# One PSUM pool of eight banks, five sets of seven products in each later group, and a tabled order, in a fused attention and gated FFN kernel

## The chip, the cores and the metric

The kernel runs on one core of a Trainium2 chip. The metric is device time in microseconds for one execution. The kernel before takes 313.35 us, the median of three runs from 313.17 to 313.43.

The engines are named as in the profile: PE is TensorE (PEld are its weight loads), DVE is VectorE, ACT is ScalarE, POOL is GpSimd, SP is the engine that issues most DMAs.

## The reference

Four batches, eight heads, 768 tokens, head size 64. Each query and key is assigned to the nearest of 16 centroids of its head; a query attends only to keys of its own cluster. The heads' outputs, side by side, are the 3072 x 512 input of an FFN with a sigmoid gate and 1536 hidden columns.

```python
q_assign = np.argmax(np.einsum('bhsd,hcd->bhsc', q_n, c_n), axis=-1)
k_assign = np.argmax(np.einsum('bhsd,hcd->bhsc', k_n, c_n), axis=-1)
mask = q_assign[:, :, :, None] == k_assign[:, :, None, :]
scores = np.where(mask, scale * np.matmul(q, k.transpose(0, 1, 3, 2)), -1000000000.0)
attn = np.exp(scores - np.max(scores, axis=-1, keepdims=True))
attn = attn / (np.sum(attn, axis=-1, keepdims=True) + 1e-09)
x = np.matmul(attn, v)          # then (b, s, h*d)
out = (1 / (1 + np.exp(-(x @ w_gate))) * (x @ w_val)) @ w_out
```

## The kernel before

**Attention.** Heads go in pairs. A pair's queries and keys are transposed (on PE at first, L617, L795, L903, later on DVE, L595), cast to 16 bits on POOL, and given 16 more rows that hold the one-hot cluster; a score matmul over 80 rows (L1008) thus adds the mask. The cluster scores come from L687, L835 and L948. An exponential on ACT (L1032) takes two score products of 384 columns at once out of two banks and writes them to one of four `es` tiles; there are 189 exponentials. The value products (L1059) take `es` as stationary operand against 65 columns of v and a column of ones, so that the sum comes with them. DVE divides (L1084, L1089), and a DMA, or PE in some blocks (L1097), transposes the result into `x`.

**FFN.** Tokens are worked in eight groups (b, gr), two of each batch, of 384 tokens (of 256 and 512 in the first batch). For each of 12 chunks of 128 hidden columns there are four matmuls with the gate weights and four with the value weights over all tokens of the group (`proj`, L1389, L1396); ACT takes tanh out of the gate's bank (L1561), DVE multiplies into `hT` (L1572). The output projection (`project`, L1186, matmuls at L1271) does two blocks of 128 tokens at a time with seven half-size products in place of eight. The sigmoid is had from tanh of half the argument.

**Seven products.** `seven_products` (L1445) does two neighbouring chunks of gate and value at once: a 2 x 2 block product with seven block products in place of eight. The blocks are halves of the input rows (`d`) and halves of the tokens (192). It needs sums of the weights, made once on DVE (`sum_up_weights`, L1366, four for each pair of chunks, in `wss`), and four differences of `x` for each group (`t_tasks`, L1436). A set is seven products of four matmuls of 192 columns (L1474), three copies out of PSUM on ACT (L1493), three additions on DVE (L1505), two tanh on ACT (L1512) and two gates on DVE (L1520). A pair of chunks done in the plain way is 16 matmuls of 384 columns, two tanh and two gates. Three banks X, Y, Z are held in a set, and X for nearly all of it: m1, copy, m6, copy, m7, addition, m4, gate. The pairs start at chunks `WP = (2, 4, 8)`; by group the kernel does 0, 0, 2, 2, 2, 3, 3, 2 sets, 14 in all. In the last group X and Y are the two banks of one score buffer.

**What sets the order.** Every piece of work is a task with an engine, an estimated duration, tasks it depends on, tile buffers (`Buf`) that it acquires or uses, and a due time. `Order.schedule` (L129) plans all tasks in a list schedule: on each engine, of those that can start within 0.02 us of the earliest, the one that is due first. The plan only fixes the order in which instructions stand on each engine, and which buffer each takes; engines then run their instructions in that order and wait on semaphores. `run` (L119) plans nine times, with DMA landing times from `transfers` (L94) between. Due times come from formulas (L319, L322).

**PSUM.** The eight banks are divided: `sc` is two buffers of two banks for scores, `av` one bank for value products, `ring` three banks for all else (L246). Buffers of `sc` and `av` are taken in turn, of `ring` the one that is free first (L70).

**DMA queues.** SP issues the loads of k, q and v (L334), the copies of half the rows to the other tile (`odd<-even`, L654), the cluster rows (`oht`), the transposes of x (L1117) and the stores; POOL issues the weights, v of later batches and some k and q.

Of the kernel before, what the change touches and what calls it, by code (L numbers as in the profile page):

```python
# [9 lines left out]
FP = mybir.dt.float32  # L10
# [3 lines left out]
AX = mybir.AxisListType  # L14

# [23 lines left out]
class Order:  # L39
# [30 lines left out]
    def free_slots(self, tag, count):  # L70

        held, got = self.held[tag], self.taken[tag]
        ends = []
# [10 lines left out]
        if tag in self.ANY:  # L84
            ends = sorted(x for x in ends if x[0] is not None)
        else:
            n = len(got) % len(held)
            ends = (ends + ends)[n : n + count]
# [5 lines left out]
    def transfers(self):  # L94


        begin = self.DMA_START
        todo = sorted((t for t in self.tasks if t.dma), key=lambda t: t.start + begin[t.eng])
        queues, left, now, n = {}, {}, 0.0, 0
        while n < len(todo) or any(queues.values()):  # L100
            heads = [ts[0] for ts in queues.values() if ts]
            come = todo[n].start + begin[todo[n].eng] if n < len(todo) else float("inf")
            if heads:
                total = sum(t.pkt for t in heads)
                step = min(min(left[t] * total / t.pkt for t in heads), max(0.0, come - now))
                for t in heads:
                    left[t] -= step * t.pkt / total
                    if left[t] < 1e-6:
                        t.landing = now + step + self.DMA_LAND - t.start
                        queues[t.eng].remove(t)  # L110
                now += step
            else:
                now = max(now, come)
            while n < len(todo) and todo[n].start + begin[todo[n].eng] <= now + 1e-9:
                queues.setdefault(todo[n].eng, []).append(todo[n])
                left[todo[n]] = todo[n].dma
                n += 1

    def run(self):  # L119

        for _ in range(8):
            order = self.schedule()
            self.transfers()
        order = self.schedule()
        for t in order:
            t.emit()
        return order

    def schedule(self):  # L129
# [10 lines left out]
        while any(wait.values()):  # L140
            best = None
            for e, ts in wait.items():
                cand = []
                for t in ts:
                    r = t.ready
                    for tag in {b.tag for b in t.acq}:
                        f = self.free_slots(tag, sum(b.tag == tag for b in t.acq))[0]
# [18 lines left out]
            wait[t.eng].remove(t)  # L166
            free[t.eng] = start + t.dur
# [21 lines left out]
            for tag in dict.fromkeys(b.tag for b in t.acq):  # L189
                mine = [b for b in t.acq if b.tag == tag]  # L190
                for b, slot in zip(mine, self.free_slots(tag, len(mine))[1]):
# [18 lines left out]
def kernel(  # L210
# [45 lines left out]
        "xn": ([128, QCH, 128], HP), "x": ([128, NDC, 512], HP), "hT": ([128, NFC, 512], HP),  # L256
        "gt": ([128, 512], FP), "p5": ([128, 384], FP), "out2": ([128, 2, DM], FP),
        "sc": ([128, 2, 512], FP), "av": ([128, 512], FP), "ring": ([128, 512], FP),
    }
    PSUM = bass.MemoryType.PSUM  # L260
    SPACES = {"sc": PSUM, "av": PSUM, "ring": PSUM}
# [4 lines left out]
            (banks if tag in SPACES else const).tile(*SHAPES[tag], name=f"{tag}{i}")  # L266
            for i in range(n)
        ]
        for tag, n in BUFS.items()
    }  # L270
    for tag, (of, which) in HEIRS.items():
# [5 lines left out]
    def take(buf):  # L277
        buf.tile = kept[buf.tag][buf.slot]
        return buf.tile

# [12 lines left out]
    WP = (2, 4, 8)  # L293
    wss = const.tile([128, len(WP), 4, 2, 2, 128], HP, name="wss")
# [56 lines left out]
    w_ring = Buf("av")  # L351
# [66 lines left out]
    c_ring = Buf("av")  # L418
# [160 lines left out]
    def prepare(b, grp, due, step, act=(), queues=("SP",), split=False):  # L579
# [101 lines left out]
        rg = Buf("sc")  # L681

        def scored():
            ps = take(rg)
# [9 lines left out]
            due, lat=0.3, acq=[rg], uses=[t32[x] for x in sides],  # L694
        )
        for half in range(2):
# [10 lines left out]
            def back(cols=cols, oh=oh, half=half):  # L707
# [5 lines left out]
                lambda t1=t1, half=half: turn_scores(take(t1)[:n], rg.tile[:n, half, :QB]),  # L713
                [cl], due, lat=0.11, acq=[t1], uses=[rg],
# [268 lines left out]
    def attend(block, at, slot):  # L983
# [11 lines left out]
        sc, es = Buf("sc"), Buf("es")  # L995
# [714 lines left out]
```

## Time and profile before

| | us |
|---|---|
| median of three runs | 313.35 |
| the profiled execution | 313.22 |
| its span, first to last instruction | 311.4 |
| busy PE, ACT, DVE, POOL in the span | 303.7, 238.2, 217.8, 77.0 |
| DMA, mean rate over the span | 111 GB/s |

The view by stretches gives for each window of the span how long each engine was busy, then the granted clock (1.00 is full), the share of the DMA engines and GB/s. The groups give, behind line, engine and operation, output and inputs with their shapes, count, then busy time and mean duration of one in ns, and the idle time before. Recorded durations of one engine overlap, so what an instruction takes from its engine is read from start to start in the timeline (start, duration), or from the chain, where each piece stands with the time it adds. Weight loads run beside matmuls.

### The profile page before, as it was taken

To read this page: it belongs to the slowest core of one execution; us is meant where nothing else is said; L and a number is where in the kernel's file an instruction comes from. 1 tells how busy PE (TensorE), PEld (TensorE's weight loads), DVE (VectorE), ACT (ScalarE), POOL (GpSimd) and SP (SyncE) were. 2 spreads that over 40 slices of the span, in tenths; PEclk is the share of its full clock that TensorE was granted. 3 is DMA by queue.
4 is the path that set the end of the run, shared out by engine and by line. 5 is a ranking of instruction groups with operands and counts; after the bars stand their busy time and mean duration, and the time that the engine had idled before them with its cause. 6 is when DMAs were issued, how large, how long until landed. Compare 5 with 4: busy or idle time off the path is not lost.

```text
span 311.4 us, 8300 instructions
## 1 busy us (share of the span) xinstructions
PE 303.7 (98%) x3251; PEld 222.8 (72%) x3251; DVE 217.8 (70%) x532; ACT 238.2 (76%) x389; POOL 77.0 (25%) x110
## 2 busy tenths in 40 slices
PE   8998999999999999999999999999999999999995
PEld 3676888544687867757776877757777888778784
DVE  4999945899865739885376938977375824685862
ACT  4799999334999989868997777959899778945531
POOL 4997756751012302440002200570000000000000
PEclk9999999999999999999999999999999999999999
DMA  6999999993356966891465673978300121001003
GB/s 217 359 272 212 214 175 129 163 154 72 69 99 142 114 100 204 106 114 45 107 105 84 101 182 99 103 101 73 96 4 14 48 83 46 15 2 67 2 1 135
DMA packets 97286, 34.49 MB, mean 111 GB/s; under 512 B 83120, under 2 KB 93024, under 8 KB 97248
## 3 DMA queue, kind: packets, MB, share of 16 engines
q1 hardware_dynamic: 72192, 24.57, 34.6%
q0 software_dynamic: 24336, 8.65, 26.4%
q10 hardware_dynamic: 720, 0.75, 0.7%
q8 instruction: 25, 0.41, 0.6%
q14 instruction: 13, 0.11, 0.2%
HBM read 28.34 MB, written 6.29 MB: 111 GB/s over the span
## 4 chain that ended last, share of the span: by engine, by line
PE 92%; ACT 4%; DVE 1%; DMA 1%; issue 0%; SPq 0%; ACTq 0%
PE ring L1396 29%; PE sc L1008 19%; PE ring L1271 16%; PE av L1059 11%; PE ring L1474 9%; ACT es L1032 3%; PE sc L687 3%; PE sc L1271 1%; PE sc L1474 1%; DMA nat<-in_k_dram 1%; PE ring L795 1%; PE ring L617 1%; PE ring L835 1%; PE ring L903 0%; PE ring L948 0%
## 5 line engine op out<-in xcount | busy, mean ns | idle before, releaser
L1032 ACT ACTIVATE es<-sc,nbias 128x768 f16<-128x768 f32 (+1 forms) x189 | 167.8, 925 | 21.2 <-PE sc L1008 20.4
L1059 PEld LDWEIGHTS <-es 128*128 128x128 f16 x1152 | 53.6, 97 | 13.6
L1059 PE MATMUL av<-vp,es 128*128 128x65 f16 x1152 | 58.6, 193 | 0.0
L1396 PE MATMUL ring<-x,wv 128*128 128x384 f16 (+2 forms) x272 | 55.4, 326 | 0.1
L1396 PE MATMUL ring<-x,wg 128*128 128x384 f16 (+2 forms) x272 | 55.3, 326 | 0.0
L1561 ACT ACTIVATE gt<-ring 128x384 f32<-128x384 f32 (+2 forms) x68 | 33.9, 499 | 28.0 <-PE ring L1396 24.8
L1572 DVE SCALAR_TENSOR_TENSOR hT<-gt,ring 128x384 f16<-128x384 f32 (+2 forms) x68 | 37.2, 548 | 24.3 <-PE ring L1396 20.7
L650 POOL CAST even<-t 128x768 f16<-128x768 f32 x24 | 20.6, 875 | 119.9 <-DVE t L595 47.1
L1396 PEld LDWEIGHTS <-wv 128*128 128x128 f16 x272 | 24.7, 97 | 16.5 <-issue 2.1
L1396 PEld LDWEIGHTS <-wg 128*128 128x128 f16 x272 | 24.4, 97 | 14.6 <-issue 0.8
L1271 PEld LDWEIGHTS <-hT 128*128 128x128 f16 x294 | 27.3, 97 | 5.0
L1008 PE MATMUL sc<-even 80*128 80x384 f16 (+2 forms) x120 | 26.1, 293 | 1.6 <-ACT es L1032 0.9
L1008 PE MATMUL sc<-odd 80*128 80x384 f16 x96 | 26.6, 325 | 0.1
L1271 PE MATMUL ring<-wo,hT 128*128 128x256 f16 x198 | 26.4, 272 | 0.0
L1008 PE MATMUL sc<-even,odd 80*128 80x384 f16 (+2 forms) x120 | 26.1, 293 | 0.0
L1008 PE MATMUL sc<-odd,even 80*128 80x384 f16 x96 | 25.8, 326 | 0.0
L1008 PEld LDWEIGHTS <-even 80*128 80x128 f16 x216 | 19.7, 98 | 8.2 <-issue 3.1
L1008 PEld LDWEIGHTS <-odd 80*128 80x128 f16 x216 | 19.7, 98 | 7.3 <-issue 2.1
L595 DVE STREAM_TRANSPOSE t<-nat 128x384 f32<-128x384 f32 x40 | 21.1, 553 | 1.2 <-DMA nat<-in_q_dram 0.9
L1505 DVE TENSOR_TENSOR nat<-ring,nat 128x384 f32<-128x384 f32 x26 | 13.9, 548 | 10.8 <-ACT nat L1493 9.2
L1296 DVE SCALAR_TENSOR_TENSOR out<-ring,diff 128x256 f32<-128x256 f32 x22 | 9.3, 422 | 17.0 <-PE ring L1271 16.8
L1271 PEld LDWEIGHTS <-s 128*128 128x128 f16 x198 | 18.7, 97 | 3.4
(133 smaller groups left out, 444.8 us busy)
## 6 DMA issues: line engine op xcount, KB each, us to landing
out_dram<-out SPq DMA_DIRECT2D x22, 256.0 KB, 2.2
nat<-in_k_dram SPq DMA_DIRECT2D x32, 96.0 KB, 3.0
nat<-in_q_dram SPq DMA_DIRECT2D x32, 96.0 KB, 3.0
odd<-even SPq DMA_DIRECT2D x12, 192.0 KB, 2.9
vp<-in_v_dram POOLq DMA_DIRECT2D x24, 96.0 KB, 4.6
nat<-in_k_dram SPq DMA_DIRECT2D x5, 384.0 KB, 7.7
nat<-in_q_dram SPq DMA_DIRECT2D x5, 384.0 KB, 6.2
nat<-in_v_dram SPq DMA_DIRECT2D x4, 384.0 KB, 7.9
```

Source lines behind the costliest of these rows:

```text
L595: nc.vector.transpose(t[:, half * QB : (half + 1) * QB].rearrange("p (c x) -> p c x", x=128), blocks_[:, half],)
L650: nc.gpsimd.tensor_copy(t[:, NM[nm], cols], t32[p, nm].tile[:, cols])
L687: nc.tensor.matmul(out=ps[32 * g : 32 * g + 32, half, :QB], lhsT=cblk[:, 2 * p + half, :], rhs=t32[p, nm].tile[:, half * QB : (half + 1) * ...
L1008: nc.tensor.matmul(out=to, lhsT=kb.tile[0:80, 0, e * QB + j // 2 * 128 : e * QB + (j // 2 + 1) * 128], rhs=qb_.tile[0:80, 1, e * QB + c0 * ...
L1032: i = nc.scalar.activation(to, of, AF.Exp, bias=nbias, scale=D ** -0.5 if quarters(b, p) else scale,).ins
L1059: nc.tensor.matmul(out=av.tile[:, g : g + D + 1], lhsT=es.tile[:, i * N + c * 128 : i * N + (c + 1) * 128], rhs=vp[:, e, j, :], start=firs ...
L1271: nc.tensor.matmul(out=ps[:, lo:hi], lhsT=left_()[:, i], rhs=right(i)[:, lo:hi], start=new and i == 0, stop=i == NFC // 2 - 1, skip_group_ ...
L1396: nc.tensor.matmul(out=ps[:, :N], lhsT=ws[fc // FPG][:, dcc, fc % FPG, :], rhs=xb.tile[:, dcc, :N], start=(dcc == 0), stop=(dcc == NDC - 1),)
L1474: nc.tensor.matmul(out=ps[:, f], lhsT=w_[:, d, f], rhs=x_()[:, d], start=new and not (f or d), stop=d == 1, skip_group_check=True,)
L1505: lambda: nc.vector.tensor_tensor(held(i), bank(r_, y), held(i), ALU.add), deps,
L1561: lambda rg=rg, gt=gt: nc.scalar.activation(take(gt)[:, :N], rg.tile[:, :N], AF.Tanh, scale=0.5),
L1572: nc.vector.scalar_tensor_tensor(t[:, fc, :N], gt.tile[:, :N], 1.0, rv.tile[:, :N], ALU.add, ALU.mult)
```

## The change

Three things change together.

1. **PSUM.** All eight banks form `ring`. A single bank is the free one whose neighbours are least useful as a pair; scores, and the cluster scores of L687, take any two neighbouring banks. `sc` (2) and `av` (1) stay as turns without memory: still at most two score pairs and one value bank are under way. The last group's sets and projections use single banks as well.
2. **Five sets** for each group of the batches 1 to 3 (`WP = (2, 4, 6, 8, 10)`), none in batch 0: 30 sets. To make room for the sums of five pairs, one of the four sums of each (g1 - v1) is written over the value weights v1 themselves, after the last plain product that reads them (`raw_users`), and the first `hT` tile is cut from 512 to 384 columns.
3. **The order.** The due times are no longer formulas: `PLACES` gives every task a rank, and `LANDINGS` every DMA a planned time; `transfers` goes. `schedule` keeps its rules, so buffers and dependencies work as before.

The numbers of instructions that differ, in the built programs: matmuls of L1396 with 384 columns 352 to 96, matmuls of L1474 392 to 840 (weight loads alike), copies of L1493 42 to 90, L1512 28 to 60, L1561 with 384 columns 44 to 12, additions of L1505 42 to 90, gates of L1520 28 to 60, L1572 with 384 columns 44 to 12, weight sums 12 to 20. Nothing else differs in number; the DMAs of SP, ACT and POOL are the same ones in another order.

```diff
...
+            till = [float("inf") if e is None else e for e, _ in ends]
+            if count == 2:
+                pairs = [(max(pair), i) for i, pair in enumerate(zip(till, till[1:]))]
+                end, i = min(pairs)
+                return (None, None) if end == float("inf") else (end, [i, i + 1])
+            soon = max(min(till), now)
+            beside = [min(till[max(i - 1, 0) : i] + till[i + 1 : i + 2]) for i in range(len(till))]
+            i = max((i for i, e in enumerate(till) if e <= soon), key=lambda i: (beside[i], -i))
+            return (None, None) if till[i] == float("inf") else (till[i], [i])
...
-        for _ in range(8):
-            order = self.schedule()
-            self.transfers()
+        places, landings = ([float(x) for x in text.split()] for text in (PLACES, LANDINGS))
+        moved = [t for t in self.tasks if t.dma]
+        assert len(places) == len(self.tasks) and len(landings) == len(moved)
+        for t, at in zip(self.tasks, places):
+            t.due = at
+        for t, landing in zip(moved, landings):
+            t.landing = landing
         order = self.schedule()
...
-        "sc": 2, "av": 1, "ring": 3, "p5": 2,
+        "ring": 8, "p5": 2, "sc": 2, "av": 1,
...
-    WP = (2, 4, 8)
-    wss = const.tile([128, len(WP), 4, 2, 2, 128], HP, name="wss")
+    WP = (2, 4, 6, 8, 10)
+    wss = const.tile([128, len(WP), 3, 2, 2, 128], HP, name="wss")
...
-        sc, es = Buf("sc"), Buf("es")
+        turn_, sc, es = Buf("sc"), [Buf("ring") for _ in range(2)], Buf("es")
...
-            avb[block] = Buf("av")
-        av = avb[block]
+            avb[block] = Buf("ring"), Buf("av")
+        av, in_av = avb[block]
...
-            r1, r2 = Buf("sc"), Buf("sc")
-            X, Y, Z = (lambda: r1.tile[:, 0, :HM]), (lambda: r2.tile[:, 0, :HM]), (lambda: r1.tile[:, 1, :HM])
...
+        r1, r2 = Buf("ring"), Buf("ring")
+        X, Y, Z = (lambda: r1.tile[:, :HM]), (lambda: r2.tile[:, :HM]), (lambda: r1.tile[:, HM:])
...
-        for to, x, y, op in (
-            (s1, v1, v2, ALU.add), (s3, g1, v1, ALU.subtract), (s2, s1, g1, ALU.subtract), (s4, g2, s2, ALU.subtract),
+        for to, x, y, op, raw in (
+            (s1, v1, v2, ALU.add, []), (s2, s1, g1, ALU.subtract, []), (s4, g2, s2, ALU.subtract, []),
+            (v1, g1, v1, ALU.subtract, raw_users[fa] + raw_users[fa + 1]),
         ):
...
-        seven = WP[: {(0, 0): 0, (0, 1): 0, (1, 0): 2, (1, 1): 2, (2, 0): 2, (2, 1): 3, (3, 0): 3, (3, 1): 2}[b, gr]]
-        if (b, gr) == (B - 1, 1):
-            seven = (2, 4)
-        if not wsums_of:
+        seven = WP if b else ()
+        if seven and not wsums_of:
...
-            if (b, gr) == (B - 1, 1):
-                X = Y = Buf("sc")
-            else:
-                X, Y = Buf("ring"), Buf("ring")
-            Z = Buf("ring")
+            X, Y, Z = Buf("ring"), Buf("ring"), Buf("ring")
...
             rv, v1 = proj("v", fc, due, [g1])
+            raw_users[fc].append(v1)
...
```

More of the change, by code (lines that the diff above doesn't have):

```diff
@@ L68, in behind, with free_slots @@
             t.left += 1
[L70 removed]
+    def free_slots(self, tag, count, now=0.0):
         held, got = self.held[tag], self.taken[tag]
@@ L166, in schedule @@
             wait[t.eng].remove(t)
+            now = max(t.ready, free[t.eng])
             free[t.eng] = start + t.dur
```

126 lines of the change are left out of this document (54 added, 72 removed), and 104 rows, old and new, of tables (LANDINGS, PLACES).

## The prediction

> **What bounds the kernel now.** I read the page's busy line first, then its clock row, then the chain that ended last.
>
> ```profile
> span 311.4 us, 8300 instructions
> PE 303.7 (98%) x3251; PEld 222.8 (72%) x3251; DVE 217.8 (70%) x532; ACT 238.2 (76%) x389; POOL 77.0 (25%) x110
> PEclk9999999999999999999999999999999999999999
> PE 92%; ACT 4%; DVE 1%; DMA 1%; issue 0%; SPq 0%; ACTq 0%
> ```
>
> TensorE (PE) carries 92% of the chain at full clock. The view by stretches tells where this holds and who else is near; behind the stretch and its length stand the busy times of PE, weight loads, DVE, ACT and POOL.
>
> ```profile
> 20.00:50.00 30.00, 28.92 (x400) 23.92 (x399) 23.38 (x67) 29.68 (x42) 20.48 (x28) 1.00 1.38 187
> 60.00:80.00 20.00, 20.00 (x111) 9.02 (x110) 19.37 (x44) 8.38 (x14) 7.56 (x10) 1.00 0.92 129
> 110.00:300.00 190.00, 189.19 (x2030) 141.88 (x2029) 130.63 (x300) 149.55 (x255) 21.56 (x26) 1.00 0.44 77
> ```
>
> From 20 to 50 us ScalarE (ACT) is full (29.68 of 30): there the exponentials set the time, PE waits a little. From 110 to 300, where every group with seven-product sets is worked, PE is full and ACT and VectorE (DVE) have 40 and 59 us to spare. A busy PE is not PE at peak, so I looked in the chain for what a group of matmuls really takes, and in the waits for what stops PE:
>
> ```profile
> 119.18 0.65 PE ring L1396 x4
> 120.16 0.66 PE ring L1474 x8
> 124.01 0.37 PE av L1059 x12
> ```
>
> ```profile
> 75.20 0.86 PE ring L1396 x4
> 132.00 1.43 PE sc L687 x16
> 302.37 1.31 PE ring L1271 x12
> ```
>
> ```profile
> PE sc L1008 <- ACT es L1032: 0.9, 2, 0.5
> PE sc L1474 <- DVE nat L1505: 0.5, 1, 0.5
> ```
>
> Four matmuls of 384 columns take 0.65 us (0.1625 each), eight of 192 take 0.66 (0.0825 each): time goes by columns. The three rows of the second fence are used below: four matmuls of 512 columns, 16 of the cluster scores (L687), twelve of 256 columns (0.109 each). PE waited for an exponential for 0.9 us in all. So a column less on PE is time less, unless the work added on ACT and DVE makes PE wait.
>
> **The change, part by part.** I counted the instructions of the changed kernel, form by form, against those of before. Only this differs in number; all else is the same work in another order.
>
> PE: 256 matmuls of 384 columns go (352 become 96, L1396), 448 of 192 columns come (392 become 840, L1474). That is 14 sets of seven products before and 30 after; a set is 28 small matmuls for 16 large ones. Sum: 256 x 0.1625 = 41.6 us away, 448 x 0.0825 = 37.0 us more: **-4.6 us**. Nothing covers PE here, so all of it counts.
>
> A small matmul brings a weight load of its own, 192 more in number (448 for 256).
>
> ```profile
> L1474 PEld LDWEIGHTS <-wss 128*128 128x128 f16 x224 | 19.1, 97 | 2.8 <-issue 0.6
> ```
>
> A load is recorded with 97 ns, longer than the 82.5 of its matmul. If loads bound, the 448 would cost 448 x 0.097 = 43.5, and the part would be +1.9 us. But eight pairs already take 0.66 us, and the twelve of L1059, each with a load of 128 columns too, 0.37: loads pass every 31 ns. I take -4.6. The Trainium skill ("TensorE: Matmul & The Clock Gate", section LDWEIGHTS) gives a load as columns / 1.2 ns, about 107 ns for 128 columns; taken as a bound of each pair that would make this part an estimated 47.9 - 41.6 = +6.3 us and the change a loss. The trace disagrees by the two chain rows.
>
> ACT: a set adds three copies and turns its two tanh of L1561 into two of L1512, so 48 copies and 32 L1512 come, 32 L1561 go.
>
> ```profile
> L1493 ACT COPY nat<-ring 128x384 f32<-128x384 f32 x24 | 12.2, 508 | 0.4 <-PE ring L1474 0.4
> L1512 ACT ACTIVATE nat<-nat 128x384 f32<-128x384 f32 x28 | 15.3, 560 | 0.8 <-DVE nat L1505 0.8
> L1561 ACT ACTIVATE gt<-ring 128x384 f32<-128x384 f32 x44 | 22.0, 501 | 12.0 <-PE ring L1396 10.7 <-DVE hT L1572 0.8
> 121.07 0.51 ACT L1493 COPY nat<-ring 128x384 f32<-128x384 f32 x1
> 121.43 0.53 ACT L1493 COPY p<-ring 128x384 f32<-128x384 f32 x1
> 121.80 0.96 ACT L1032 ACTIVATE es<-sc,nbias 128x768 f16<-128x768 f32 x1
> 122.60 0.53 ACT L1493 COPY nat<-ring 128x384 f32<-128x384 f32 x1
> 122.95 0.60 ACT L1512 ACTIVATE nat<-nat 128x384 f32<-128x384 f32 x1
> 123.38 0.96 ACT L1032 ACTIVATE es<-sc,nbias 128x768 f16<-128x768 f32 x1
> ```
>
> By durations this is 48 x 0.508 + 32 x (0.560 - 0.501) = +26.3 us. But instructions overlap: in the timeline (start, duration) copies follow each other by 0.36, an exponential takes 0.80 from start to start, a tanh 0.43. With 0.40 for L1561, between copy and tanh, ACT really gets 48 x 0.36 + 32 x 0.03 = +18.2 us. The Trainium skill ("Perfetto Trace Analysis", section Optimizing Scalar/DVE Operations) says that the write acknowledgement of an instruction overlaps the next one; the rows agree (0.51 recorded, 0.36 apart).
>
> DVE: 48 additions come (L1505), the gates stay 32 for 32 at equal length, and eight more weight sums (20 for 12) come.
>
> ```profile
> L1505 DVE TENSOR_TENSOR nat<-ring,nat 128x384 f32<-128x384 f32 x26 | 13.9, 548 | 10.8 <-ACT nat L1493 9.2 <-PE ring L1474 1.4
> L1377 DVE TENSOR_TENSOR wss<-wv 128x512 f16<-128x512 f16 x3 | 1.2, 414 | 0.0
> 123.27 0.54 DVE L1505 TENSOR_TENSOR nat<-ring,nat 128x384 f32<-128x384 f32 x1
> 123.73 0.55 DVE L1505 TENSOR_TENSOR p<-ring,p 128x384 f32<-128x384 f32 x1
> 299.14 0.36 DVE L1241 TENSOR_TENSOR s<-hT 128x384 f16<-128x384 f16 x1
> 299.41 0.35 DVE L1241 TENSOR_TENSOR nat<-hT 128x384 f16<-128x384 f16 x1
> ```
>
> 48 x 0.46 + 8 x 0.414 = +25.4 us.
>
> What hides these? From 110 to 300 us ACT goes from 150 to 168 and DVE from 131 to 153, in a stretch that PE now fills in 185. On average they fit. Locally I laid the three orders side by side: from the scores of one exponential to the value products of a later one, how much has PE to do, how much ACT? The tightest stretches of the changed kernel, by the paces above (score matmuls like L1396, 0.031 for a value product, and 0.28 for a halving of L1289, an estimate from the copy's 0.36 by columns, rounded up):
> - exponentials 88 to 99: PE 136 x 192 columns, 28 x 384, 84 value products, 8 of L687: 19.1 us; ACT 12 x 0.80 + 15 x 0.36 + 10 x 0.43 = 19.3.
> - 111 to 120: PE 68 x 192, 20 x 384, 18 x 256, 60 value products: 12.7; ACT 10 x 0.80 + 6 x 0.36 + 6 x 0.43 + 0.28 = 13.0.
> - 127 to 129: 4.0 against 4.0.
>
> To ACT comes the way from PE and back, about 0.3 us (an exponential's 0.96 less 0.80, and as much for a matmul's tail). So PE lacks 0.5, 0.6 and 0.3 us. The bounds are 0 (before, the same count lacks up to 0.3 in places and PE waited only 0.9 in all) and 3 (six groups with 0.5 each); I take **+0.8**.
>
> Pool and pairs: the eight banks were 2 x 2 for scores, 1 for values, 3 for products; now any free bank or pair serves. No instruction is added. What it removes are waits for banks, and PE shows almost none. I take 0; bounds -0.5 (the two wait rows are halved) and +0.5 (a pair found later).
>
> Order: the table puts 12 more exponentials ahead of the long block of 512-column products (57 for 45). In that stretch the changed order gives ACT 12 exponentials and five tanh of 256 and 512 columns, about 11 us, and PE 24 score, 72 value and 40 product matmuls, also about 11: ACT stays the bound longer, PE loses nothing by it. I take **-0.3**, since scores and values alternate more finely there; bounds -2 (ACT's few idle spots and PE's 1.1 us of the first stretch go, and the same again earlier) and +1. DMAs are the same in number on SP, ACT and POOL. Moved past them are k, q loads and the shift copies; what DMAs cost now:
>
> ```profile
> DVE t L595 <- DMA nat<-in_q_dram: 0.9, 1, 0.9
> ```
>
> DVE waited 0.9 us, not PE: 0, up to +1. The five subtractions that now write over the value weights stand among the gates of group (0,1), whose products read those weights: DVE from 60 to 80 us is full (19.37 of 20), so 5 x 0.41 = 2 us come where DVE has no room, less what the table moved out. Queued behind a waiting one are gates, on which banks hang. PE's 24 products there take 24 x 0.86 = 20.6 us. I take 0; bounds 0 and +2.
>
> Tail: the last group has five sets where it had two.
>
> ```profile
> 276.80 0.33 PE L1097 MATMUL ring<-ident,xn 128*128 128x128 f16 x3 [0.25 <-DVE hT L1520]
> 288.00 0.49 PE L1474 MATMUL sc<-nat,wss 128*128 128x192 f16 x4 [0.50 <-DVE nat L1505]
> 306.82 0.83 PE L1271 MATMUL sc<-nat,hT 128*128 128x128 f16 x12
> ```
>
> After the last transposes (L1097) PE has 148 x 192, 57 x 256 and 16 x 384 columns up to its last small product: 21 us. DVE up to its last gate has 16 additions, 14 gates and 4 long sums at 0.46, 4 differences, 8 short sums and 3 results at about 0.27 (the rows of L1241): 15.6 + 4.1 = 20 us. Nearly equal, with chains between. Before, this stage lost about 1 us (68 x 384, 120 x 256, 56 x 192 and 12 x 128 columns, 29.4 us, between 277.2 and 307.65). I take 0 over that; bounds -1 and +2.5.
>
> Sum: -4.6 + 0.8 - 0.3 = -4.1. The profiled execution took 313.22 us (span 311.4 and 1.8 around it), 0.13 under the median of 313.35: 309.1, or **309.2** beside the median.
>
> **The rivals.**
> - *Sets wait (slower).* In a set X's bank goes product, copy, product, copy, product, addition, product. A copy behind an exponential on ACT waits up to 0.80. If 15 of the 30 sets have no other work for PE at two such places, 0.2 us each, that is +6.0: 313.2 - 4.6 - 0.3 + 6.0 = 314.3. It decides from 0.16 us a set (4.9 / 30). Against it: 14 sets now cost PE 0.5 us. For it: ACT is at 95% of PE where the sets stand.
> - *The tail is DVE's.* 2.5 us more, 311.7. For it: 20 against 21 us. Against it: before, DVE idled there.
> - *The start gains more.* -2 in place of -0.3: 307.4, and without the 0.8 306.6.
> - *Loads bound.* 313.2 + 1.9 + 0.5 = 315.6; the two chain rows speak against it.
>
> **How the numbers follow.** Forecast 0.70 (307.6 to 311.0), sets wait 0.12, tail 0.10, start 0.05, loads 0.03. The range from 307.0 to 312.2 holds forecast and tail and leaves out the others. A difference of 0.2% (0.6 us) is about what can be told from none. Faster: forecast, tail, start: 0.85. Slower: sets wait and loads, less the weak end of the former: 0.13; same 0.02.
>
> **What would show it.** L1474 x840 at 0.66 per eight, L1396 of 384 columns x96; PE busy near 299; PE's waits for L1032, L1493 and L1505 together under 3 us; ACT about 168 from 110 to 300. Wrong, if eight small products take over 0.7, if PE waits for copies in each group, or if the tail from L1097 on is over 31 us.

## The result, and the profile after

| | us |
|---|---|
| kernel before, median of 19 runs | 313.61 (313.17 to 314.86) |
| changed kernel, median of 19 runs | 311.50 (309.14 to 318.07) |
| ratio | 0.9925, 95% interval 0.9909 to 0.9942 |
| the same ratio in a later group of runs | 0.9934, interval 0.9919 to 0.9949 |

The change makes the kernel faster by 1.8 to 2.85 us, 2.35 in the middle; on the profiled execution of before (313.22) that is 310.9. The forecast was 309.2: the sign and the range hold, but only some 60% of the 4.1 us came. The profile of the 318.07 us run is not used below, because its granted clock fell to 0.5 twice between 35 and 50 us, for 3.4 us each time; "the changed kernel" below is an execution of 311.65 us from the later group.

Where lines are named, those of the changed kernel count: L1008 of before is L1111 (scores), L1032 is L1135 (exponentials), L1396 L1497 (plain products), L1474 L1570 (set products), L1493 L1589 (copies), L1505 L1601 (additions), L1512 L1608 (a set's tanh), L1561 L1657 (plain tanh), L1572 L1669 (plain gates), L1117 L1220 (transposes by DMA), L1377 L1478 (weight sums). Kernels with inserted lines shift these a little.

The page of the changed kernel: span, busy times, granted clock, shares of the chain that ended last.

```profile
span 309.9 us, 8785 instructions
PE 299.7 (97%) x3443; PEld 234.0 (76%) x3443; DVE 241.8 (78%) x588; ACT 255.4 (82%) x437; POOL 77.0 (25%) x110
PEclk9999999999999999999999999999999999999998
PE 84%; ACT 7%; DVE 4%; DMA 3%; issue 1%; DVEq 0%; ACTq 0%
```

TensorE (PE) has fallen from 92% to 84% of the chain: there is less of it, and others stand in it that did not before. The chain shows the pace of the new work, the groups its number.

```profile
121.91 0.66 PE ring L1570 x8
```

```profile
L1570 PE MATMUL ring<-nat,wv 128*128 128x192 f16 x240 | 28.9, 246 | 0.0
L1497 PE MATMUL ring<-x,wg 128*128 128x384 f16 x48 | 9.9, 326 | 1.1 <-DMA x<-xn 1.1
```

Eight small products take 0.66 us as before, and the idle time stands in front of a plain product, behind a DMA. The view by stretches (busy PE, weight loads, DVE, ACT, POOL) of before and of the changed kernel tells where PE is idle:

```profile
50.00:70.00 20.00, 20.00 (x169) 11.61 (x166) 15.97 (x37) 9.02 (x17) 13.78 (x18) 1.00 1.25 157
160.00:220.00 60.00, 60.00 (x640) 43.45 (x638) 44.34 (x104) 47.43 (x77) 13.43 (x16) 1.00 0.69 105
```

```profile
50.00:70.00 20.00, 18.59 (x225) 13.45 (x223) 15.04 (x36) 17.71 (x27) 12.86 (x17) 1.00 1.41 160
160.00:220.00 60.00, 58.43 (x701) 46.50 (x700) 51.71 (x122) 53.89 (x96) 13.14 (x16) 1.00 0.70 103
110.00:300.00 190.00, 188.43 (x2270) 157.56 (x2269) 153.51 (x355) 169.68 (x309) 22.78 (x28) 1.00 0.45 73
```

PE stands still for 1.4 us between 50 and 70, and 1.6 between 160 and 220, where before it did not. The waits of PE in the changed kernel (total, times, longest) name what ended them:

```profile
PE ring L1111 <- ACT es L1135: 1.6, 5, 0.4
PE ring L1497 <- DMA x<-xn: 1.1, 1, 1.1
PE ring L1497 <- DVE hT L1669: 0.8, 1, 0.8
PE ring L1111 <- issue: 0.6, 1, 0.6
```

One wait for a transposed block, one for one gate, five short ones for exponentials, and one in front of scores for which the profile names nothing (its place and cause follow under `again`).

To compare kernels that do the same work at other times I made a ledger from the starts of all matmuls in the trace. Each matmul is given its usual step (0.2165 us for 512 columns, 0.1625 for 384, 0.109 for 256, 0.0825 for 192, 0.056 for 128, 0.031 for 65; 0.09 and 0.109 for the 32-bit ones of 384 and 128); the start of a matmul less the steps of all before it is PE's lost time up to there. The steps add up to 296.0 us before and 291.4 in the changed kernel: **PE's work fell by 4.6**. The lost time, by stretches of the clock (columns in us of the trace; the steps are rounded, so single entries hold to about 0.1 and sums to about 0.2):

| kernel | to 30 | 30-50 | 50-70 | 70-110 | 110-160 | 160-220 | 220-260 | 260 to end | sum |
|---|---|---|---|---|---|---|---|---|---|
| before | 7.6 | 1.0 | 0.1 | 0.3 | 0.5 | 0.3 | 0.3 | 1.6 | 11.7 |
| changed | 7.6 | 1.2 | 1.8 | 0.2 | 0.6 | 2.6 | 0.2 | 0.4 | 14.6 |
| again | 7.6 | 2.3 | 2.2 | -0.1 | 1.0 | 2.5 | 0.2 | 0.4 | 16.1 |
| late_sums | 7.6 | 1.2 | 1.9 | 0.7 | 1.8 | 1.8 | 0.1 | 0.3 | 15.4 |
| no_table | 8.4 | 2.4 | 0.7 | 0.2 | 1.0 | 6.1 | 1.1 | 5.5 | 25.4 |
| pool_only | 7.5 | 2.4 | 0.7 | 0.4 | 0.3 | 0.4 | 0.3 | 0.2 | 12.2 |
| sets_only | 7.6 | 1.0 | 0.1 | 0.5 | 2.5 | 5.9 | 2.6 | 11.7 | 31.9 |
| gap_sums | 7.6 | 1.2 | 1.1 | 0.2 | 0.7 | 2.6 | 0.2 | 0.2 | 13.8 |
| tanh_quarter | 7.6 | 1.2 | 1.1 | 0.2 | 0.3 | 1.7 | 0.2 | 0.3 | 12.6 |
| gate_first | 7.7 | 1.9 | 0.0 | 0.2 | 0.8 | 2.1 | 0.2 | 0.4 | 13.3 |
| projection_later | 7.9 | 1.3 | 0.4 | 0.2 | 0.7 | 2.2 | 0.1 | 0.5 | 13.3 |
| mended | 7.6 | 1.1 | 0.0 | 0.2 | 0.7 | 2.2 | 0.2 | 0.2 | 12.2 |
| mended_tanh_quarter | 8.5 | 1.3 | 0.2 | 0.2 | 0.3 | 1.7 | 0.1 | 0.1 | 12.4 |

So the question is where 2.9 us more lost time (14.6 less 11.7) come from: 1.7 at 50 to 70 us, 2.3 at 160 to 220, 0.2 at 30 to 50, and 1.2 given back in the tail.

### The profile page after: what moved, and what is told of

Same layout as the page of the kernel before. It is cut to its first block, busy times and chain, and to the rows that moved or that the text cites. A ratio compares the mean times of both kernels' runs of the same rounds, so it can differ in the third digit from the quotient of the medians.

```text
span 316.3 us, 8785 instructions
## 1 busy us (share of the span) xinstructions
PE 302.6 (96%) x3443; PEld 236.0 (75%) x3443; DVE 241.2 (76%) x588; ACT 255.4 (81%) x437; POOL 76.5 (24%) x110
## 4 chain that ended last, share of the span: by engine, by line
PE 75%; DMA 11%; ACT 4%; POOL 4%; DVE 2%; SPq 2%; issue 1%; DVEq 0%; POOLq 0%; ACTq 0%
PE ring L1570 18%; PE ring L1372 17%; PE ring L1111 15%; PE ring L1497 15%; PE ring L1162 9%; DMA wv<-in_moe_w_val_dram 5%; DMA nat<-in_v_dram 2%; ACT es L1135 2%; PE ring L791 2%; SPq L438 2%; DMA x<-xn 2%; POOL odd L927 1%; POOL even L927 1%; DMA cn<-in_centroids_dram 1%; ACT nat L1608 1%
## 5 line engine op out<-in xcount | busy, mean ns | idle before, releaser
L1135 ACT ACTIVATE es<-ring,nbias 128x768 f16<-128x768 f32 (+1 forms) x189 | 167.2, 928 | 13.8 <-PE ring L1111 7.2
L1162 PE MATMUL ring<-vp,es 128*128 128x65 f16 x1152 | 57.6, 196 | 0.1
L1601 DVE TENSOR_TENSOR nat<-ring,nat 128x384 f32<-128x384 f32 x60 | 32.8, 552 | 12.7 <-PE ring L1570 5.9
L1608 ACT ACTIVATE nat<-nat 128x384 f32<-128x384 f32 x60 | 32.2, 552 | 3.5 <-DVE nat L1601 3.5
L1657 ACT ACTIVATE gt<-ring 128x256 f32<-128x256 f32 (+2 forms) x36 | 17.7, 497 | 19.2 <-PE ring L1497 13.6
L1570 PEld LDWEIGHTS <-wss 128*128 128x128 f16 x360 | 30.5, 98 | 3.3 <-issue 0.6
L1589 ACT COPY nat<-ring 128x384 f32<-128x384 f32 x60 | 29.9, 503 | 3.8 <-PE ring L1570 3.4
L1497 PE MATMUL ring<-x,wg 128*128 128x256 f16 (+2 forms) x144 | 29.2, 328 | 3.8 <-DVE x L1216 2.9
L1497 PE MATMUL ring<-x,wv 128*128 128x256 f16 (+2 forms) x144 | 29.4, 330 | 0.0
L1570 PE MATMUL ring<-nat,wv 128*128 128x192 f16 x240 | 29.0, 246 | 0.0
L1570 PE MATMUL ring<-x,wg 128*128 128x192 f16 x240 | 28.8, 246 | 0.0
L1570 PE MATMUL ring<-nat,wss 128*128 128x192 f16 x240 | 28.3, 246 | 0.0
L1111 PE MATMUL ring<-even,odd 80*128 80x384 f16 (+2 forms) x120 | 27.5, 296 | 0.5 <-ACT es L1135 0.4
L1111 PE MATMUL ring<-even 80*128 80x384 f16 (+2 forms) x120 | 27.2, 296 | 0.7 <-POOL vp L625 0.4
L1669 DVE SCALAR_TENSOR_TENSOR hT<-gt,ring 128x256 f16<-128x256 f32 (+2 forms) x36 | 19.5, 547 | 10.9 <-PE ring L1497 9.2
L1111 PE MATMUL ring<-odd,even 80*128 80x384 f16 x96 | 27.0, 333 | 0.7 <-ACT es L1135 0.7
L1111 PE MATMUL ring<-odd 80*128 80x384 f16 x96 | 26.9, 328 | 0.0
L1111 PEld LDWEIGHTS <-even 80*128 80x128 f16 x216 | 19.4, 99 | 8.0 <-issue 4.7
```

Of the source, the lines that this page charges most:

```text
L1111: nc.tensor.matmul(out=to, lhsT=kb.tile[0:80, 0, e * QB + j // 2 * 128 : e * QB + (j // 2 + 1) * 128], rhs=qb_.tile[0:80, 1, e * QB + c0 * ...
L1135: i = nc.scalar.activation(to, of, AF.Exp, bias=nbias, scale=D ** -0.5 if quarters(b, p) else scale,).ins
L1162: nc.tensor.matmul(out=av.tile[:, g : g + D + 1], lhsT=es.tile[:, i * N + c * 128 : i * N + (c + 1) * 128], rhs=vp[:, e, j, :], start=firs ...
L1497: nc.tensor.matmul(out=ps[:, :N], lhsT=ws[fc // FPG][:, dcc, fc % FPG, :], rhs=xb.tile[:, dcc, :N], start=(dcc == 0), stop=(dcc == NDC - 1),)
L1570: nc.tensor.matmul(out=ps[:, f], lhsT=w_[:, d, f], rhs=x_()[:, d], start=new and not (f or d), stop=d == 1, skip_group_check=True,)
L1589: nc.scalar.copy(held(i), bank(r_))
```

## The experiments

Theory A: single places of the new order, where an awaited instruction stands behind one that takes longer, or lands later, than the table supposed. Theory B: more sets bring ScalarE (ACT) so near its limit that PE waits for it throughout the later groups. Each kernel was run beside the kernel before, which took 313.3 to 313.5 in every group; ratios are to it.

### again, late_sums: is VectorE held by a late weight load?

> The changed kernel once more, for a profile. Theory A (DVE stands behind a weight sum that waits for a weight load, and PE behind DVE; how long differs from run to run with the landing of the load): the wait of the sums of L1478 on the load of wv is again there between 33 and 45 us, but shorter than the 4.9 us of the first profile, by about as much as the time is under 318; from 60 us on the trace takes as long as in the first profile. Theory B (the additional sets make PE wait for ACT and DVE in the later groups, more than the 0.8 us forecast): the time over the forecast lies behind 110 us.

The changed kernel with nothing edited, one execution: 313.13 us. Its timeline shows the suspected chain, on VectorE (DVE) and then on PE:

```profile
34.76 0.41 DVE L1478 TENSOR_TENSOR wss<-wv 128x512 f16<-128x512 f16 x1
36.62 0.43 DVE L1478 TENSOR_TENSOR wss<-wv 128x512 f16<-128x512 f16 x1 [1.45 <-DMA wv<-in_moe_w_val_dram]
38.60 0.39 DVE L1216 CAST x<-ring 128x256 f16<-128x256 f32 x1
39.04 0.60 PE L1497 MATMUL ring<-x,wg 128*128 128x256 f16 x4 [0.97 <-DVE x L1216]
```

The bracket is idle time in front of an instruction and what ended it. A weight sum stands 1.45 us for its load; two more sums, two transpositions and the cast behind it come late; PE waits 0.97 us for the cast. The waits of PE in this execution hold that one, and one for the copies of the cluster rows:

```profile
PE ring L1111 <- DMA even<-oht: 1.2, 1, 1.2
PE ring L1497 <- DVE x L1216: 1.0, 1, 1.0
```

The wait for the cluster rows is also in the execution of 311.65 us, where it is the one without a name. The first row is of `again`, the second of that execution:

```profile
57.38 0.48 PE L1111 MATMUL ring<-even 80*128 80x384 f16 x2 [1.18 <-DMA even<-oht]
55.78 0.48 PE L1111 MATMUL ring<-even 80*128 80x384 f16 x2 [0.63 <-issue]
```

In `again` the last `even<-oht` copy was issued at 51.61 us and landed 5.7 us later, at 57.29, 0.09 before PE went on. In the other one it was issued at 50.62 and landed 5.1 us later, at 55.69, again 0.09 before PE went on. late_sums has the same wait (0.8 us); the six profiles of the later runs that keep the table (gap_sums, tanh_quarter, gate_first, projection_later, mended, mended_tanh_quarter) do not have it. Why the landing varies stays open.

So the wait that theory A names is there, but `again` also loses 2.7 us more than the kernel before between 110 and 220 us, where theory B looks for the loss. One execution does not decide between them.

> Only the eight weight sums that read the second third of the weights move on DVE, from between 35 and 90 us to behind 98 us, ahead of their first use; every other engine keeps its order. Theory A: PE no longer waits at 33 to 45 us, the time falls by about 2 us to about 309.5 (0.987 of before) and its spread over runs shrinks. Theory B: no change against the changed kernel (0.9925), or up to 1 us more, since DVE has the sums where it feeds PE.

```diff
+            if t.eng == "DVE" and t.start >= 98.0 and late:
+                n += 1
+                if n % 2 == 0:
+                    order_.append(late.pop(0))
+            order_.append(t)
...
+        if fa // FPG == 1:
+            for t in tasks:
+                t.late = True
```

312.56 us median (311.23 to 316.14, 12 runs), ratio 0.998, interval 0.9959 to 1.0: the gain of theory A did not come. The loss at 30 to 50 us is 1.2 instead of 2.3, but 110 to 160 grew to 1.8 and 70 to 110 to 0.7: there the sums stand in front of DVE work that PE waits for. The gain was spent in the new place, and more: by the ratios (0.998 here, 0.9934 for the changed kernel in change_timed) the kernel is some 1.4 us slower than the changed one, over the 1 us that theory B allowed. gap_sums, below, puts the sums better.

### no_table, pool_only, sets_only: the parts alone

> One pool and five sets as in the change, but due times by the old formulas and landing times by the old estimate in place of the table. Theory A: the table itself brought the wait; the formulas leave the sums where the loads have landed, but they were fitted to 14 sets, so PE waits more in the later groups: 310 to 314. Theory B (sets cost, whatever the order): 313 or more.

```diff
-        places, landings = ([float(x) for x in text.split()] for text in (PLACES, LANDINGS))
...
+        for _ in range(8):
+            order = self.schedule()
+            self.transfers()
         order = self.schedule()
```

321.97 us (321.23 to 322.84), ratio 1.027, interval 1.0252 to 1.0288. Theory A missed by 8 us; theory B has the sign, but not "whatever the order", since the same sets in the written order take 311.5.

> One pool of eight banks, with the old 14 sets, formulas and landing estimates. Both theories: PE did not wait for banks before, so 313.6, within 0.5 us of before; if the pool by itself takes away waits it is up to 1 us faster, if pairs come late up to 1 us slower.

```diff
-    WP = (2, 4, 6, 8, 10)
+    WP = (2, 4, 8)
-        seven = WP if b else ()
+        seven = WP[: {(0, 0): 0, (0, 1): 0, (1, 0): 2, (1, 1): 2, (2, 0): 2, (2, 1): 3, (3, 0): 3, (3, 1): 2}[b, gr]]
```

(besides the formulas of before, and a fourth sum in `wss` as before). 313.87 us (313.47 to 314.52), ratio 1.0015, interval 1.0005 to 1.0024, within the 0.5 us expected. The ledger shows two effects in it: the tail loses 0.2 us in place of 1.6, and 30 to 70 us lose 3.1 in place of 1.1.

> Only the sets: five of seven products in every later group on the pools of the kernel before (score pairs in fixed banks), with its formulas for the order and no table. PE's work falls by 4.7 us as in the changed kernel. The formulas with the one pool gave 322.0 us, 8.5 above the kernel before. If the pool carries the sets (without it the sets have five buffers for 30 sets of three banks), this is worse still: 323 to 328. If the missing table alone was the loss, it is the same: 321 to 323. If the one pool had made it worse, 314 to 320.

```diff
-    WP = (2, 4, 8)
+    WP = (2, 4, 6, 8, 10)
...
-        seven = WP[: {(0, 0): 0, (0, 1): 0, (1, 0): 2, (1, 1): 2, (2, 0): 2, (2, 1): 3, (3, 0): 3, (3, 1): 2}[b, gr]]
+        seven = WP if b else ()
```

(on the kernel before, with the sum over v1 that the change brings). 328.73 us (328.55 to 329.16), ratio 1.0489, interval 1.0473 to 1.0504, slightly over the highest case. Two of PE's waits in sets_only, then its stretch from 110 to 300 us (ACT is the fourth busy time), then the same stretch of no_table:

```profile
PE sc L1474 <- ACT p L1493: 1.4, 3, 0.7
PE sc L1474 <- DVE nat L1505: 1.3, 3, 0.6
```

```profile
110.00:300.00 190.00, 183.93 (x2128) 146.92 (x2127) 140.88 (x318) 157.78 (x286) 21.57 (x26) 1.00 0.43 76
```

```profile
110.00:300.00 190.00, 185.38 (x2184) 150.60 (x2181) 143.57 (x323) 161.74 (x295) 22.10 (x26) 1.00 0.43 76
```

PE idles 6.1 and 4.6 us there, with ACT doing less than the 169.68 of the changed kernel: so ACT is not full. What PE waits for is mixed: the named waits for copies and additions of sets (L1493 and L1505 in sets_only) come to 5.2 us in sets_only, all but 0.3 of them behind 260 us, and to 2.4 in no_table; those for exponentials come to 2.5 and 2.7. That is part of the 20.2 and 13.7 us that these two lose more than the kernel before; the rest lies in gates, a transpose and many small gaps. The three runs give prices: the pool alone +0.5 us; 30 sets on it under the formulas +8.1 on top (322.0 less 313.9); without the pool they cost 6.7 more (328.7 less 322.0); the table takes away 10.5 (322.0 to 311.4).

### change_timed, gap_sums, tanh_quarter

> The changed kernel again, as the yardstick of this group of runs. Both theories: 0.9925 of the kernel before in the first series, so about 311.0 us where that one takes 313.4. The single execution of it in the first group took 313.1, so its executions may lie widely apart: theory A (VectorE stands behind a weight sum that waits for a weight load) expects that, from 310 to 315, because the landing of that load differed by 5 us between two executions; theory B (ScalarE and VectorE are late for the sets of the later groups, which is the same work in every execution) expects them within 1 us.

The changed kernel, unedited: 311.44 us (310.99 to 311.84, 6 runs), ratio 0.9934. This group of executions lay within 1 us, as theory B has it; the first had spread from 309.1 to 313.0.

> The eight weight sums of the two blocks whose weights come with the second load are moved on VectorE out of 35 to 45 us: three into stretches at 82, 83.5 and 86 us of the plan where VectorE idles at least 0.5 us, five into the stretch at 104 to 107 us where it idles 3.6 us. Nothing else is moved. Before, moving them to 98 to 110 us took 1.1 us off PE's lost time at 30 to 50 us and put 1.1 us on at 110 to 120. Theory A: 1 to 2 us less than the changed kernel in the same group (309.5 to 310.5), and PE's lost time at 50 us about 8.8 instead of 9.9 us or more. Theory B: within 0.3 us of the changed kernel.

```diff
+        spots = [82.0, 83.5, 86.0] + [107.0] * 5
...
+            while t.eng == "DVE" and spots and t.start >= spots[0]:
+                spots.pop(0)
+                order_.append(late.pop(0))
+            order_.append(t)
...
+        if fa // FPG == 1:
+            for t in tasks:
+                t.late = True
```

311.18 us (310.89 to 312.44), ratio 0.9934, interval 0.9917 to 0.9951: no difference from the changed kernel beside it. The sums cost nothing in the idle stretches (70 to 160 us as in the changed kernel), but at 30 to 50 us there was nothing to save, since the load came in time in that execution of the changed kernel (1.2 lost with either). The late load is a loss of some executions; that it makes the spread of the first series was not shown.

> ScalarE's 60 tanh of the sets, in place on 384 columns, are done on the first 96 columns only, so that three quarters of those gates are left without their tanh; every other instruction is as in the changed kernel. At about 0.24 us less for each of them ScalarE does 14 us less work, spread over 120 to 290 us, near the 18 us that the change had added. Theory B (ScalarE late in the later groups): the 2.5 us of PE's lost time that came between 110 and 220 us go, so 2 to 2.5 us less than the changed kernel. Theory A: below 0.5 us.

```diff
-                    lambda: nc.scalar.activation(held(i), held(i), AF.Tanh, scale=0.5), [m], due_ffn(work), lat=0.16,
+                    lambda: nc.scalar.activation(held(i)[:, : N // 4], held(i)[:, : N // 4], AF.Tanh, scale=0.5), [m], due_ffn(work), lat=0.16,
```

```profile
L1608 ACT ACTIVATE nat<-nat 128x96 f32<-128x96 f32 x60 | 17.1, 291 | 5.0 <-DVE nat L1601 4.8
```

ACT's busy time fell by 9.6 us (255.4 to 245.8). 310.79 us (309.58 to 312.53), ratio 0.992, interval 0.9893 to 0.9946: by the times alone between the theories. The ledger has 0.3 and 1.7 lost at 110 to 160 and 160 to 220, for 0.6 and 2.6: 1.2 us less. Of this 0.35 is a shorter wait for a transposed block (0.73 for 1.08, at 210 us), so some 0.85 us of the extra loss are ScalarE's.

### gate_first, projection_later, mended

The wait for a gate at 63.6 us in the changed kernel, its timeline on the three engines:

```profile
60.41 0.41 DVE L1270 TENSOR_TENSOR nat<-wo 128x512 f16<-128x512 f16 x1
60.86 1.56 DVE L1271 TENSOR_TENSOR wo<-wo 128x512 f16<-128x512 f16 x1
61.30 0.83 POOL L754 CAST even<-t 128x768 f16<-128x768 f32 x1
62.35 0.41 DVE L1270 TENSOR_TENSOR nat<-wo 128x512 f16<-128x512 f16 x1
63.13 0.41 DVE L1669 SCALAR_TENSOR_TENSOR hT<-gt,ring 128x256 f16<-128x256 f32 x1
63.60 1.02 PE L1497 MATMUL ring<-x,wg 128*128 128x512 f16 x4 [0.78 <-DVE hT L1669]
```

A subtraction of the output weights that elsewhere takes 0.42 us takes 1.56, while GpSimd (POOL) casts. The gate stands behind it and behind one more pair, and PE stands for the gate's bank. The pair that is moved next is the second one, 62.35 to 63.21 us; the slow sum belongs to the first pair, which stays.

> One subtraction pair of the output weights, which ran 1.03 to 1.98 us on VectorE between 61 and 63 us while GpSimd's casts ran, is moved behind the gating product, the transposition, the reciprocal and the normalization that stood after it; nothing else moves. In the changed kernel PE waits 0.78 us at 63.6 us for that gating product. Theory A (single places of the order, where the awaited instruction stands behind one that the plan had as shorter or as landed): that wait falls to 0 to 0.2 us, PE's lost time at 70 us from 10.6 to 9.9 us, the time by 0.5 to 0.8 us to about 310.8 where the kernel before takes 313.4. Theory B (ScalarE's pace in the later groups): no change, within 0.2 us of the changed kernel, since later waits are what they are.

```diff
         order = self.schedule()
+        for what, behind in ((575, 592),):
+            first = next(t for t in order if t.due == what)
+            i = order.index(first)
+            j = order.index(next(t for t in order if t.due == behind)) + 1
...
+            order[i:j] = [t for t in order[i:j] if t not in moved] + moved
```

Rank 575 is the second pair of L1270 and L1271 on DVE, 592 the normalization; `moved` is the task and what between depends on it.

```profile
60.83 0.42 DVE L1280 TENSOR_TENSOR wo<-wo 128x512 f16<-128x512 f16 x1
61.44 0.42 DVE L1678 SCALAR_TENSOR_TENSOR hT<-gt,ring 128x256 f16<-128x256 f32 x1 [0.18 <-PE ring L1506]
62.62 1.03 PE L1506 MATMUL ring<-x,wg 128*128 128x512 f16 x4
```

The gate is done at 61.86, PE passes without a wait, and nothing is lost from 50 to 70 us. 310.31 us (309.93 to 311.1), ratio 0.9905, interval 0.989 to 0.9921: theory A's direction, and 0.5 us below its 310.8. Two things in this execution are not the move's doing: the cluster rows landed in time, and the first pair, which kept its place, ran beside no cast at 0.42 us a sum, which by itself would have brought the gate in time. mended_tanh_quarter, below, has the move with a slow first pair (60.57 to 62.60 us):

```profile
60.57 1.07 DVE L1290 TENSOR_TENSOR nat<-wo 128x512 f16<-128x512 f16 x1
61.67 0.93 DVE L1291 TENSOR_TENSOR wo<-wo 128x512 f16<-128x512 f16 x1
62.52 0.41 DVE L1692 SCALAR_TENSOR_TENSOR hT<-gt,ring 128x256 f16<-128x256 f32 x1
```

There the gate is done at 62.93, PE starts the next projection at 62.98 with no wait in front of it, and only 0.2 us are lost from 50 to 70. So the move alone takes the wait away.

At 211.9 us the changed kernel waits for a block transposed by DMA:

```profile
205.92 4.88 POOL L438 DMA_DIRECT2D vp<-in_v_dram  x6
206.66 1.20 SPq L1220 DMA_TRANSPOSE x<-xn  x1
211.92 0.32 PE L1497 MATMUL ring<-x,wg 128*128 128x384 f16 x1 [1.08 <-DMA x<-xn]
212.28 0.49 ACT L1657 ACTIVATE gt<-ring 128x384 f32<-128x384 f32 x1 [1.02 <-PE ring L1497]
```

```profile
DMA to landing us min/median/max: 2.9/4.1/5.2
```

The second view is the tile's, for 195 to 214 us: the later of two transposes took 5.2 us from issue to landing, while POOL issued six loads. The table has 2.8 for it.

> At 210 us the four matmuls of one 384-column projection, whose last one waits 1.08 us for a transposed block that lands 5.2 us after its issue, stand seven tasks later on PE (four scores, one value product, one product of a set), and its tanh behind the exponentials of those. Theory A: the wait falls below 0.2 us and the time by 0.8 to 1.0 us, to about 310.5. Theory B: PE waits for ScalarE instead, which has idled 1.02 us in the same place and then has no slack, and the gain is below 0.3 us.

```diff
+        for what, behind in ((1686, 1699),):
```

Rank 1686 is the projection on PE; its tanh on ACT goes with it.

```profile
209.48 0.48 PE L1120 MATMUL ring<-even 80*128 80x384 f16 x2 [0.17 <-ACT es L1144]
210.64 0.86 PE L1506 MATMUL ring<-x,wg 128*128 128x384 f16 x4
211.54 0.49 ACT L1666 ACTIVATE gt<-ring 128x384 f32<-128x384 f32 x1 [0.53 <-PE ring L1506]
212.08 0.81 PE L1506 MATMUL ring<-x,wg 128*128 128x384 f16 x4 [0.39 <-ACT gt L1666]
```

The DMA wait is gone, but PE now waits 0.17 for an exponential and 0.39 for the tanh, which the late product made late: 0.56 for 1.08, and the ledger shows 2.2 for 2.6 lost from 160 to 220 us. The place belongs to A, what is left of it to B. 310.54 us (310.25 to 311.85), ratio 0.9919, interval 0.9902 to 0.9936. That this meets theory A's 310.5 is luck in part: the rest of its distance to the changed kernel lies at 50 to 70 us, where it did not touch the order and this execution lost 0.4 for 1.8.

> The two moves above and the eight weight sums in VectorE's idle stretches, together. Theory A: PE's lost time at 300 us 12.2 to 12.6 instead of 14.6, the time 309.0 to 309.8, about 2 us under the changed kernel and near the forecast. Theory B: 311 to 311.4, since each place that is mended comes back as a wait for ScalarE.

```diff
+        spots = [82.0, 83.5, 86.0] + [107.0] * 5
...
+        for what, behind in ((575, 592), (1686, 1699)):
```

309.72 us (309.24 to 310.29), ratio **0.9882**, interval 0.9867 to 0.9897, with 12.2 us lost, as theory A said: below the changed kernel's interval and below that of the kernel before, the best version of this study, and 0.5 us over the forecast. Its waits of PE, with the scores at L1131, the exponentials at L1155:

```profile
PE ring L1131 <- ACT es L1155: 1.8, 6, 0.4
PE ring L483 <- PEq L1814: 0.8, 1, 0.8
PE ring L1072 <- DVE cblk L554: 0.4, 1, 0.4
PE ring L1131 <- DVE even L698: 0.4, 1, 0.4
PE ring L1520 <- ACT gt L1680: 0.4, 1, 0.4
```

Neither a DMA nor a gate of DVE is left among them; what is left in the groups is ACT.

### mended_tanh_quarter

> The three moves of mended, and the sets' tanh on the first 96 of 384 columns as in tanh_quarter, so that three quarters of those gates are left without it. In mended PE's lost time still grows by 2.8 us from 120 to 220 us, where the kernel before loses 0.7, and every wait that PE has left there is for ScalarE. Theory B for this remainder (ScalarE nearly without slack): lost time from 120 to 220 us below 1.5 us and the time 1.0 to 1.5 us under mended, 308.2 to 308.7 where the kernel before takes 313.3. If the remainder is something else, such as the single places: within 0.4 us of mended.

```diff
+        for what, behind in ((575, 592), (1686, 1699)):
...
+                    lambda: nc.scalar.activation(held(i)[:, : N // 4], held(i)[:, : N // 4], AF.Tanh, scale=0.5), [m], due_ffn(work), lat=0.16,
```

308.77 us (308.27 to 309.49, 4 runs), ratio 0.9851, interval 0.9834 to 0.9867: 1.0 us under mended, as B said for the remainder. The ledger is less clear: from 110 to 220 us 2.0 lost for 2.9, not below 1.5; the profiled execution is the slowest of the four and lost 0.9 more before 30 us. In it, 0.9 us of the 1.7 from 160 to 220 are the same two waits as in projection_later: what the late transpose left. The shorter tanh takes time from ACT and lets the set's own gate start sooner; the run does not part the two.

## Why the prediction was right, and where it was wrong

- **PE -4.6: right.** The steps add up to 4.6 less; eight small products take 0.66 us, and the rival of the weight loads (315.6) fell with them.
- **ACT and DVE load: right.** ACT 169.68 and DVE 153.51 from 110 to 300 us, where 168 and 153 were forecast. That is 90% of PE's 188.43 for ACT; the 95% named for the rival "sets wait" was a slip, since the prediction's own 168 of 185 are 91%.
- **Windows +0.8, with PE's waits below 3 us: right in size.** Taking 10 us from ACT gave 1.0 us (mended to mended_tanh_quarter), 0.9 between these two in the ledger, and 0.85 in that of tanh_quarter. ScalarE's price is about +0.9 to +1.0; PE waits for exponentials for 1.6 us, and for no copy and no addition.
- **DMAs "0, up to +1": the step that failed.** The argument was that their number is unchanged and that DVE, not PE, waited for them. But the change moved what stands behind them. The transpose issued at 206 us lands 4.5 to 5.5 us later in every profile with the table, and PE waits for it for 0.3 to 1.2 us where the projection stands in its place (1.1 in change_timed and again, 0.7 in gate_first, 0.3 in late_sums). In the kernel before, two transposes of this stretch took 5.4 and 4.7 us to land, and PE waited for neither. Two more come and go: the cluster rows (1.2 in again, 0.6 in change_timed, none in gate_first), and the weight load at 36 us (PE waits 1.0 behind it in again, 0.6 in gate_first, none in change_timed).
- **Order -0.3: wrong in sign, +0.9.** To 30 us the lost time is the same 7.6. DVE from 60 to 80 us was named as full, and gates as what would queue; but the rows that held them up were not the five subtractions over the value weights (70 to 110 us lose nothing more). They were the subtractions of the output weights, of which one or two are slow beside a cast on POOL. gate_first and mended_tanh_quarter showed that with the second pair behind the gate the wait is gone.
- **Pool 0, bounds 0.5: right for 14 sets** (+0.5), as the balance of a gain in the tail and a loss at 30 to 70 us, and no statement on 30: under the formulas, these take 6.7 us longer without the pool. Since the parts came together this did not touch the sum.
- **Tail 0: too low a gain.** Lost time from 260 us on fell from 1.6 to 0.4, -1.2; PE did not come to wait for DVE. pool_only, with two sets in the last group, has 0.2 there, so by the ledger the common pool brings this gain without the table and without the added sets; the prediction had weighed the tail by the amounts of work on PE and DVE alone.
- **Rival "sets wait": wrong for the change.** PE waits for no copy or addition of a set there. Without the table the sets do cost more than they save (322.0), but its mechanism is a part of that only, 2.4 us of named waits in no_table. That the table removed its condition, no other work for PE at these points, is a reading and not shown.

For the execution of 311.65 us the parts add up. In the ledger's amounts, which lie about 0.15 over each wait of the profile: -4.6 + 1.0 (ScalarE, 160 to 220 us) + 1.3 (transpose) + 0.9 (gate) + 0.8 (cluster rows) + 0.2 (30 to 50 us) - 1.2 (tail) = -1.6, and it took 1.57 us less than the profiled execution of before (313.22). The forecast had -4.1: 2.1 of the difference are the two DMA waits, 1.2 the order's term, and the tail gives 1.2 back. That the time lies in the forecast's range is luck in part: without the tail's gain, which was not foreseen, 311.5 would be near 312.7, over the range's 312.2. The gain over all executions is -2.1 to -2.35; that the landings that vary make the difference to the -1.6 of this one was not shown, since it would take many profiled executions.

## What to carry to other kernels

When a kernel's order is written down as a table, its price is not in the amount of work but in the few instructions that others stand behind: look for long or late ones (a load, a transpose by DMA, a sum beside GpSimd) in front of the one that the busiest engine awaits, and move those apart; two moves, and eight sums put into idle stretches (which alone gained nothing), took off 1.6 us (ratio 0.9882 for 0.9934), where the whole change had brought 2.1. A ledger of lost time by stretches shows such places even where the profile names no releaser, as at 55 us here. And work taken from the bound counts in full only where what replaces it is fed in time: the same 30 sets under the old order, with and without the common pool, made the kernel 2.7 and 4.9% slower than the kernel before.

## What the runs showed of the hardware

- A 16-bit DVE sum of 512 columns with both inputs in SBUF takes 0.42 us alone and up to 1.56 beside a GpSimd cast. In eight profiles here (before, changed, again, gap_sums, gate_first, projection_later, mended, tanh_quarter) 15 of the 24 such sums that overlap a cast take over 0.45, and eight of the other nine touch only the last 0.1 us of one; of the 109 that overlap only the issue of DMAs by GpSimd none takes over 0.43, nor of the 115 beside neither. The Trainium skill ("SBUF — State Buffer", section SBUF: two separate sides) says that such a sum and a GpSimd instruction that reads SBUF share a port pair, which the one that starts first holds for its whole instruction while the other blocks. The rows agree that one holds the other up (the sum of 1.56 us ends 0.29 after the cast). They do not show that the first one goes first: this sum is recorded from 60.86, 0.44 before the cast, and in its usual 0.42 us it would have been over.
- A transpose by DMA lands 2.3 to 5.5 us after its issue from 195 to 214 us, and the same one late in execution after execution (5.2 in change_timed and again, 4.9 in mended), each time beside six loads that GpSimd issues: it can be planned for. That the loads make it late was not tested. The second load of the value weights varies: DVE waited 1.45 us for it in again, 1.1 in gate_first, 0.5 in change_timed.
